# A fused attention and two-layer feed-forward kernel: the pooling of two key/value batches moves between engines, six steps change their number format, and the opening is reordered

## The chip, the cores and the metric

The kernel runs on one core of a Trainium2 chip. The metric is the device time of one execution in microseconds (us). TensorE (PE) multiplies matrices and writes to PSUM, VectorE (DVE), ScalarE (ACT) and GpSimd (POOL) work element by element, and SyncE (SP) issues every DMA of this kernel from one queue, in order.

## The reference

The core of what is computed (the first weights are called `moe_`, the second `moe2_`):

```python
k_p = k.reshape(B, H, Sp, 8, D).mean(axis=3)          # B, H, S, D = 8, 8, 576, 64; Sp = 72
v_p = v.reshape(B, H, Sp, 8, D).mean(axis=3)
scores = matmul(q, k_p.transpose(0, 1, 3, 2)) / sqrt(D)
attn = exp(scores - max); attn = attn / (sum(attn) + 1e-09)
x = matmul(attn, v_p)                                  # made (4608, 512): tokens by heads*64
h = x @ w_in1                                          # (4608, 2048)
g = where(h >= 1, h, where(h <= -1, 0, (h + 1)**2 / 4))
y = g @ w_out1                                         # (4608, 512)
out = (max(y @ w_in2, 0)**2) @ w_out2
```

## The kernel before

**Tiling.** The 4608 tokens are 36 attention tiles of 128 (`NTILE`), and 9 blocks of 512 (`NB`) in the first feed-forward layer. A block takes 16 steps (`KF`), one for each 128 of the 2048 inner columns. Step s multiplies the block's x by a column group of w_in1 (`gemm1`, L642, tile `ph`), turns the result into g (`step_ops`, L656), and two steps later (`LAG`) `gemm2` (L705) adds g times a row group of w_out1 into four accumulators `acc`. Steps are counted from 0. Here step 0 starts its `ph` matmuls at 42.07 us, step 3 at 62.72, step 8 at 104.91, step 13 at 145.82 and step 21 at 210.61. The second layer for all but the first block runs at the end, in another form, and is not touched.

**Number formats.** A float32 operand is either split into a high and a low part of type fp32r, and the product made of three matmuls (hi*hi, hi*lo, lo*hi), or multiplied whole, as float32. `whole` (L612) says which: `gemm2` of steps 0 to 15 is whole (L713, tile `gw`), every later one split (L724, tiles `gh` and `gl`). A split costs a ScalarE copy for the weight (L217), a VectorE subtraction for the weight (`wolo`, L221), a ScalarE copy of g (L687) and a VectorE subtraction of g (`gl`, L693).

**Weights.** The 32 tiles of w_in1 and w_out1 are staged by DMA (`st`, four buffers) and converted once: two ScalarE operations (L148, L151), three VectorE operations (L153, L156, L159) and one GpSimd addition (L162). Three tiles a step are converted up to step 5, then two, with a lead of 8 tiles (`LEAD`), so the last is converted around step 12. Then the second layer's weights follow in the same way (`prepare_w2`, tiles `z` and `cb`).

**Attention.** A tile of q is transposed (`unit_q`, L334): tiles 0 to 10 by TensorE (L347) out of rows of 64, tiles from `TURNED` = 11 on by VectorE (L338) after a load in pieces of 32 columns, 16 DMAs to a run of tokens (L253). Scores are made in two halves g (`unit_s`, L358): TensorE (L363), maximum on VectorE (L379), exp on ScalarE, the sum and the division by it in `norm` (L411). Attention weights of tiles 0 to 3 are transposed by TensorE (`unit_p`, L438), later ones go through DRAM. `unit_x` (L473) multiplies by the pooled v; its result is split (L485, L486) into the x of the block.

**Pooling.** The sum over 8 rows of k and v is made batch by batch (8 batches, each 4 loads of k and 4 of v, two heads a load). For batches below `ON_PE` = 3, TensorE sums in PSUM, by 8 accumulating matmuls (`unit_k` L301, `unit_v` L320). For the others GpSimd makes three additions, of 512, 256 and 128 elements (`pool_kv`, L290 and L291), and TensorE only transposes k (L306). A load buffer (`kvp`, three buffers) comes free when the pooling has read it.

**Order.** `before` (L495) lists by hand what the opening issues until step 0: k, q, s, p, v, x are the units above; `e` runs the exps that wait; `norm` divides; `head` and `tail` are the two halves of a weight's conversion; `hi` and `lo` split a weight. `slots` (L500) places the later units at half steps: batch 1's v at half steps 7 and 9, batch 2's k at 30 and 31 (step 15) and its v at 37 and 39 (steps 18 and 19). `pool_at` places GpSimd's pooling of the later batches. A scheduler then may move an instruction ahead of others on its engine where it is ready earlier, so the order in the trace is near to the program's, but not the same. The loads ahead of the loop are listed at L848 to L860.

Of the kernel before, what the change touches and what calls it, by code (L numbers as in the profile page):

```python
# [23 lines left out]

TURNED = 11

# [5 lines left out]
def pooled_attention_moe_moe(  # L32
# [59 lines left out]

    ON_PE = 3
    NK = -(-SP // TR)
# [183 lines left out]

    def pool_kv(nm, b, p):
        if b < ON_PE:  # L280
            return
        a = kv_t.pop((nm, b, p))
        if nm == "v":
            if p == 0:
                vp[b] = at.tile([SP, H, D], F32, tag="vp", name="vp")
            o = vp[b][:, 2 * p:2 * p + 2, :]
        else:
            o = kp[b, p] = at.tile([SP, 2, D], F32, tag="kp", name="kp", bufs=4)
        for w in (4 * D, 2 * D):
            nc.gpsimd.tensor_tensor(out=a[:, :, 0:w], in0=a[:, :, 0:w], in1=a[:, :, w:2 * w], op=ALU.add)  # L290
        nc.gpsimd.tensor_tensor(out=o, in0=a[:, :, 0:D], in1=a[:, :, D:2 * D], op=ALU.add)  # L291

    def unit_k(b, p0):
        pk = bank([P, 2, SP], "pk")
        for i in range(2):
            if b < ON_PE:

                a = kv_t.pop(("k", b, p0 + i)).rearrange("s h (r d) -> s h r d", r=POOL)
                for r in range(POOL):
                    for e in range(2):  # L300
                        nc.tensor.matmul(  # L301
                            out=pk[e * D:(e + 1) * D, i, :], lhsT=a[:, e, r, :], rhs=ident[:SP, :SP],
                            start=(r == 0), stop=(r == POOL - 1),
                        )
                continue
            nc.tensor.transpose(out=pk[:, i, :], in_=kp.pop((b, p0 + i)), identity=ident[:SP, :SP])  # L306
# [8 lines left out]
    def unit_v(b, p0):  # L315
        pv = bank([P, 2, 2, D], "pv")
        for i in range(2):
            a = kv_t.pop(("v", b, p0 + i)).rearrange("s h (r d) -> s h r d", r=POOL)
            for r in range(POOL):
                nc.tensor.matmul(  # L320
                    out=pv[:SP, i], lhsT=ident[:SP, :SP], rhs=a[:, :, r, :],
                    start=(r == 0), stop=(r == POOL - 1),
                )
# [34 lines left out]
    def unit_s(t, g):  # L358
# [8 lines left out]
        if g == 0:  # L367
            pn_t[t] = (
                early_pn(t) if t in (0, 1, 3) else at.tile([P, H, SP], F32, tag="pn", name="pn", bufs=1),
                at.tile([P, H, 1], F32, tag="mx", name="mx"),  # L370
            )
            if t in ON_ACT:
                sums[t] = at.tile([P, H, 1], F32, tag="sm", name="sm", bufs=3)
        pn, mx = pn_t[t]
        h = slice(4 * g, 4 * g + 4)
        s4 = pss.rearrange("p i (e s) -> p (i e) s", e=2)

        def evac():
            nc.vector.tensor_reduce(out=mx[:, h, :], in_=s4, axis=AX.X, op=ALU.max)  # L379
            if t in ON_ACT:  # L380
# [5 lines left out]
            nc.vector.tensor_tensor(  # L386
                out=pn[:, h, :], in0=s4, in1=mx[:, h, :].to_broadcast([P, 4, SP]), op=ALU.subtract
            )
            later.append(exp)

        def exp():
            if t in ON_ACT:
                for i in range(4 * g, 4 * g + 4):
                    nc.scalar.activation(
                        out=pn[:, i, :], in_=s4[:, i - 4 * g, :], func=AF.Exp, scale=exp_scale, bias=mx[:, i, :],
                        accum_out=sums[t][:, i, :],
                    )
                if g == 1:
                    norms.append(t)
                return  # L400
            nc.scalar.activation(out=pn[:, h, :], in_=pn[:, h, :], func=AF.Exp, scale=exp_scale)
            if g == 1:
# [4 lines left out]
    def early_pn(t):  # L407
        flat = pad[t % 3].rearrange("p n h c -> p (n h c)")
        return flat[:, 0:H * SP].rearrange("p (h s) -> p h s", h=H)

    def norm(t):  # L411
        pn, mx = pn_t[t] if t < TB0 else pn_t.pop(t)
        if t in sums:
            sm = sums.pop(t)
        else:
            sm = at.tile([P, H, 1], F32, tag="sm", name="sm", bufs=3)
            nc.vector.tensor_reduce(out=sm, in_=pn, axis=AX.X, op=ALU.add)

        nc.vector.tensor_scalar(out=sm, in0=sm, scalar1=1e-9, scalar2=float(POOL), op0=ALU.add, op1=ALU.mult)
        nc.vector.reciprocal(out=sm, in_=sm)  # L420
        if t < TB0:
            nc.vector.tensor_tensor(out=pn, in0=pn, in1=sm.to_broadcast([P, H, SP]), op=ALU.mult)
            return
        for i in range(NK):
            n = min(TR, SP - i * TR)
# [41 lines left out]
    def unit_x(t):  # L467
# [27 lines left out]
    before = (  # L495
        "k0,0 q0 s0,0 k0,2 q1 e s0,1 s1,0 e q2 s1,1 e v0,0 norm0 q3 s2,0 e s2,1 e head norm1 p0,0 p0,1"
        " v0,2 s3,0 e s3,1 e norm2 q4 p1,0 p1,1 norm3 x0 p2,0 p2,1 tail x1 p3,0 p3,1 head x2 tail hi0 x3 head tail"
        " lo hi1 lo head head"
    ).split()
    slots, pool_at = {}, {}  # L500
    for t in range(TB0, NTILE):
# [10 lines left out]
        if t in first_tile:  # L512
            b = first_tile.index(t)
            todo.update({2 * c - 2 + i // 2: ("k", b, i) for i in (0, 2)})
            if b < ON_PE:
                todo.update({at_v: ("v", b, i) for at_v, i in zip(((7, 9), (37, 39))[b - 1], (0, 2))})
            for i in range(2 * NP if b >= ON_PE else 0):
# [623 lines left out]
```

## Time and profile before

| | before |
|---|---|
| median of 3 runs | 1678.51 us (1674.55 to 1680.96) |
| the profiled execution, its own time | 1677.34 us |
| its span in the profile | 1675.5 us |
| busy: PE, DVE, ACT, POOL | 1642.8, 1219.0, 885.5, 315.7 us |
| mean granted TensorE clock | 0.994 |

The profile's page gives the share of the whole span: TensorE is busy for 98% of it, VectorE 73%, ScalarE 53%, GpSimd 19%. A busy time of TensorE holds short stalls inside its pipelined matmuls, so the stages have to be read one by one: busy time of each engine in a stretch, then who waited for whom in it, then the instructions in order of time.

### The profile page before, as it was taken

To read this page: it belongs to the slowest core of one execution; us is meant where nothing else is said; L and a number is where in the kernel's file an instruction comes from. 1 tells how busy PE (TensorE), PEld (TensorE's weight loads), DVE (VectorE), ACT (ScalarE), POOL (GpSimd) and SP (SyncE) were. 2 spreads that over 40 slices of the span, in tenths; PEclk is the share of its full clock that TensorE was granted. 3 is DMA by queue.
4 is the path that set the end of the run, shared out by engine and by line. 5 is a ranking of instruction groups with operands and counts; after the bars stand their busy time and mean duration, and the time that the engine had idled before them with its cause. 6 is when DMAs were issued, how large, how long until landed. Compare 5 with 4: busy or idle time off the path is not lost.

```text
span 1675.5 us, 23857 instructions
## 1 busy us (share of the span) xinstructions
PE 1642.8 (98%) x8096; PEld 1329.5 (79%) x8096; DVE 1219.0 (73%) x1963; ACT 885.5 (53%) x1603; POOL 315.7 (19%) x291
## 2 busy tenths in 40 slices
PE   8999999999999999999999999999999999999998
PEld 7666787778788787878788888888888888887886
DVE  5997478888788788888876462569557856985585
ACT  6664455656566566666566542346435533553353
POOL 1443245243514425232240000000000000000000
PEclk9999999999999999999999999999999999999999
DMA  9674534534344445443553085567687777677675
GB/s 241 168 229 156 156 83 139 163 98 142 102 150 135 119 135 171 125 129 109 181 179 117 7 299 172 170 194 231 191 253 219 207 208 239 212 209 228 194 207 133
DMA packets 276728, 284.72 MB, mean 170 GB/s; under 512 B 151168, under 2 KB 179840, under 8 KB 276608
## 3 DMA queue, kind: packets, MB, share of 16 engines
q1 hardware_dynamic: 276608, 283.21, 56.5%
q8 instruction: 65, 1.06, 0.3%
q14 instruction: 55, 0.45, 0.1%
HBM read 218.10 MB, written 65.01 MB: 169 GB/s over the span
## 4 chain that ended last, share of the span: by engine, by line
PE 71%; DVE 5%; POOL 2%; issue 1%; DMA 1%; ACT 1%; SPq 0%; DVEq 0%; POOLq 0%; ACTq 0%
PE ph L652 17%; PE acc L724 17%; PE dp L999 10%; PE cp L990 10%; PE dq L999 5%; PE cr L990 5%; PE dr L999 3%; PE cq L990 2%; PE px L473 1%; PE pss L363 1%; DMA w<-w2i 1%; DVE wolo L221 1%; DVE gl L693 1%; POOL z L162 1%; DVE wilo L221 1%
## 5 line engine op out<-in xcount | busy, mean ns | idle before, releaser
L652 PE MATMUL ph<-xhi,wihi 128*128 128x512 f32 x576 | 232.8, 404 | 2.7 <-DVE g L685 2.7
L652 PE MATMUL ph<-xhi,wilo 128*128 128x512 f32 x576 | 226.4, 393 | 0.0
L652 PE MATMUL ph<-xlo,wihi 128*128 128x512 f32 x576 | 226.1, 392 | 0.0
L947 ACT ACTIVATE gh<-g 128x512 fp32r<-128x512 f32 x224 | 139.1, 630 | 149.2 <-DVE g L1016 48.0
L724 PE MATMUL acc<-gh,wohi 128*128 128x512 f32 x512 | 206.3, 403 | 2.5 <-DVE o L738 1.5
L724 PE MATMUL acc<-gh,wolo 128*128 128x512 f32 x512 | 201.1, 393 | 3.9 <-DVE wolo L221 3.9
L724 PE MATMUL acc<-gl,wohi 128*128 128x512 f32 x512 | 200.5, 392 | 0.0
L990 PE MATMUL cp<-x,w 128*128 128x512 f32 x768 | 186.2, 390 | 0.2
L754 DVE TENSOR_TENSOR gl<-g,gh 128x512 fp32r<-128x512 f32 x224 | 151.5, 689 | 47.7 <-ACT gh L947 45.9
L990 PEld LDWEIGHTS cp<-x,w 128*128 128x128 f32 x768 | 143.9, 188 | 31.3 <-ACT s L1012 1.4
L999 PE MATMUL dp<-gh,w 128*128 128x512 f32 x512 | 161.6, 389 | 0.0
L221 DVE TENSOR_TENSOR wilo<-wi,wihi 128x512 fp32r<-128x512 f32 x144 | 114.8, 797 | 62.3 <-ACT wihi L217 62.1
L693 DVE TENSOR_TENSOR gl<-g,gh 128x512 fp32r<-128x512 f32 x144 | 116.3, 808 | 56.5 <-ACT gh L687 53.9
L217 ACT ACTIVATE wihi<-wi 128x512 fp32r<-128x512 f32 x144 | 90.1, 626 | 92.3 <-PE ph L652 91.8
L652 PEld LDWEIGHTS ph<-xhi,wihi 128*128 128x128 f32 x576 | 109.0, 190 | 32.3 <-DVE g L685 4.0
L687 ACT ACTIVATE gh<-g 128x512 fp32r<-128x512 f32 x128 | 80.5, 629 | 96.2 <-DVE g L685 95.7
L652 PEld LDWEIGHTS ph<-xhi,wilo 128*128 128x128 f32 x576 | 108.8, 189 | 23.3
L652 PEld LDWEIGHTS ph<-xlo,wihi 128*128 128x128 f32 x576 | 109.2, 190 | 22.0 <-issue 0.7
L290 POOL TENSOR_TENSOR kv<-kv 72x512 f32<-72x512 f32 x80 | 92.5, 1158 | 156.2 <-DMA kv<-in_v_dram 79.7
L1012 ACT ACTIVATE s<-cp 128x512 f32<-128x512 f32 x96 | 57.1, 595 | 118.8 <-PE cp L990 118.1
L724 PEld LDWEIGHTS acc<-gh,wolo 128*128 128x128 f32 x512 | 96.6, 189 | 23.4 <-DVE wolo L221 4.9
L724 PEld LDWEIGHTS acc<-gh,wohi 128*128 128x128 f32 x512 | 96.6, 189 | 23.3 <-DVE o L738 2.0
(142 smaller groups left out, 3206.7 us busy)
## 6 DMA issues: line engine op xcount, KB each, us to landing
w<-w2i SPq DMA_DIRECT2D x224, 256.0 KB
w<-w2o SPq DMA_DIRECT2D x224, 256.0 KB
w2i<-cb SPq DMA_DIRECT2D x32, 512.0 KB
w2o<-cb SPq DMA_DIRECT2D x32, 512.0 KB
st<-in_moe_w_out_dram SPq DMA_DIRECT2D x31, 512.0 KB
st<-in_moe_w_in_dram SPq DMA_DIRECT2D x29, 512.0 KB
pd<-pad SPq DMA_DIRECT2D x32, 384.0 KB
z<-pd SPq DMA_DIRECT2D x96, 128.0 KB
```

The lines of the kernel that those rows point to most:

```text
L217: nc.scalar.activation(out=hi, in_=src, func=AF.Copy)
L221: eng.tensor_tensor(out=lo, in0=src, in1=hi.bitcast(F32), op=ALU.subtract)
L290: nc.gpsimd.tensor_tensor(out=a[:, :, 0:w], in0=a[:, :, 0:w], in1=a[:, :, w:2 * w], op=ALU.add)
L652: nc.tensor.matmul(out=ph, lhsT=a[:, kk % a.shape[1], :], rhs=c[:, kk, :], start=(i == 0), stop=(i == 3 * KD - 1))
L687: act(out=gh, in_=g, func=AF.Copy)
L693: nc.vector.tensor_tensor(out=gl, in0=g, in1=gh.bitcast(F32), op=ALU.subtract)
L724: nc.tensor.matmul(out=o, lhsT=lhsT, rhs=rhs, start=(f == 0 and x == 0), stop=(f == KF - 1 and x == 2),)
L754: tt(out=out, in0=a, in1=b, op=ALU.subtract)
L947: act(out=hi, in_=a, func=AF.Copy)
L990: nc.tensor.matmul(out=out[0], lhsT=w[:, a, k, :], rhs=xq[b, i][c][:, k, :], start=(n == 0 and i in (1, 2, 7)), stop=(n == 5), skip_group_ ...
L999: nc.tensor.matmul(out=out[d], lhsT=w[:, a, d, :], rhs=x[c], start=(g == 0 and n == 0 and i in (1, 2, 7, 4)), stop=(g == NG - 1 and n == 2 ...
L1012: act(out=snaps[key], in_=a, func=AF.Copy)
```

## The change

Seven edits go together. (1) `ON_PE` is 2: batch 2 is pooled by GpSimd in the way of the later batches, and its slots follow: the pooling of its k is issued at half steps 16, 18, 20 and 22 (steps 8 to 11), of its v at 32, 34, 36 and 38 (steps 16 to 19). (2) Batch 0 gets two of its three additions ahead of TensorE, k on VectorE and v on GpSimd; TensorE then sums 2 rows and not 8. (3) `WHOLE` = 10: `gemm2` of steps 10 to 15 is split. (4) `TURNED` is 8: q tiles 8, 9 and 10 are loaded in pieces and turned by VectorE. (5) Tile 3's attention weights lie in two buffers of the tag `gl` that the loop doesn't use yet, and not in tile 0's, so its scores needn't wait until tile 0's weights are transposed; the small buffers `mx` and `sm` become four. (6) `before` puts the scores of all four tiles ahead of the values v and of the products x, and the first conversion later. (7) q tiles 1 to 3 are loaded ahead of v.

```diff
+WHOLE = 10
-TURNED = 11
+TURNED = 8
-    ON_PE = 3
+    ON_PE = 2
     def pool_kv(nm, b, p):
+        if b == 0:
+            a = kv_t[nm, b, p]
+            for w in (4 * D, 2 * D):
+                (nc.vector if nm == "k" else nc.gpsimd).tensor_tensor(
+                    out=a[:, :, 0:w], in0=a[:, :, 0:w], in1=a[:, :, w:2 * w], op=ALU.add
+                )
         if b < ON_PE:
             return
...
-                for r in range(POOL):
+                n = 2 if b == 0 else POOL
+                for r in range(n):
...
-                            start=(r == 0), stop=(r == POOL - 1),
+                            start=(r == 0), stop=(r == n - 1),
...
-            pn_t[t] = (
-                early_pn(t) if t in (0, 1, 3) else at.tile([P, H, SP], F32, tag="pn", name="pn", bufs=1),
...
+            if t == 3:
+                pn = [gp.tile([P, H // 2, SP], F32, tag="gl", name="pn") for _ in range(2)]
...
-        "k0,0 q0 s0,0 k0,2 q1 e s0,1 s1,0 e q2 s1,1 e v0,0 norm0 q3 s2,0 e s2,1 e head norm1 p0,0 p0,1"
-        " v0,2 s3,0 e s3,1 e norm2 q4 p1,0 p1,1 norm3 x0 p2,0 p2,1 tail x1 p3,0 p3,1 head x2 tail hi0 x3 head tail"
-        " lo hi1 lo head head"
+        "k0,0 q0 s0,0 q1 k0,2 e s0,1 s1,0 e q2 s1,1 e s2,0 q3 norm0 e s2,1 e s3,0 norm1 e s3,1 e p0,0 p0,1 norm2"
+        " v0,0 head p1,0 p1,1 v0,2 x0 norm3 p2,0 p2,1 tail head x1 q4 p3,0 p3,1 x2 tail hi0 head x3 tail lo hi1 lo head head"
...
     def whole(kind, s):
-        return kind == "o" and s < KF
+        return kind == "o" and s < WHOLE
...
     load_kv_to(NP)
-    load_q_to(2)
+    load_q_to(3)
     load_kv_to(2 * NP)
-    load_q_to(3)
```

## Rows read from the trace of the kernel before

**Rows 1.** Busy time by stretch: from:to length, each engine's busy us (instructions), PEclk, DMA share, GB/s
```profile
0.00:23.43 23.43, 18.92 (x198) 17.92 (x199) 4.00 (x12) 8.48 (x30) 1.77 (x9) 1.00 0.89 205
23.43:42.07 18.64, 15.92 (x170) 14.67 (x168) 18.37 (x37) 17.30 (x46) 5.73 (x6) 0.89 1.00 285
...
104.91:145.82 40.91, 37.26 (x163) 23.36 (x160) 37.02 (x62) 21.45 (x40) 17.70 (x14) 1.00 0.61 178
145.82:210.61 64.79, 64.79 (x422) 47.59 (x421) 36.70 (x64) 32.61 (x63) 17.78 (x18) 1.00 0.53 159
```

**Rows 2.** TensorE's waits in steps 8 to 12: waiter, releaser: us, times, longest
```profile
PE pss L363 <- DVE xlo L486: 3.7, 2, 2.3
```

**Rows 3.** Timeline of TensorE, steps 13 to 19: start, us, instruction
```profile
149.18 3.60 PE L713 MATMUL acc<-gw,wo 128*128 128x512 f32 x8
152.73 0.50 PE L652 MATMUL ph<-xhi,wihi 128*128 128x512 f32 x1
...
155.59 0.60 PE L347 MATMUL pq<-ident,q 128*128 128x128 f32 x4
156.03 3.60 PE L713 MATMUL acc<-gw,wo 128*128 128x512 f32 x8
...
163.53 2.22 PE L301 MATMUL pk<-ident,kv 72*64 72x72 f32 x64
165.68 3.70 PE L713 MATMUL acc<-gw,wo 128*128 128x512 f32 x8
...
189.29 0.48 PE L724 MATMUL acc<-gh,wohi 128*128 128x512 f32 x1
...
192.13 3.66 PE L320 MATMUL pv<-kv,ident 72*72 72x128 f32 x32
195.54 0.48 PE L652 MATMUL ph<-xhi,wihi 128*128 128x512 f32 x1
```

**Rows 4.** Timeline of TensorE, a later batch pooled by GpSimd
```profile
274.15 0.29 PE L306 MATMUL pk<-ident,kp 72*128 72x72 f32 x2
```

**Rows 5.** VectorE groups, 230 to 300 us: shapes, count, busy, mean ns, idle before
```profile
L221 DVE TENSOR_TENSOR wolo<-wo,wohi 128x512 fp32r<-128x512 f32 x11 | 11.6, 1056 | 0.3 <-ACT wohi L217 0.3
L693 DVE TENSOR_TENSOR gl<-g,gh 128x512 fp32r<-128x512 f32 x10 | 10.0, 1000 | 2.9 <-ACT gh L687 2.8
...
L338 DVE STREAM_TRANSPOSE qT<-q 128x512 f32<-128x512 f32 x3 | 2.1, 698 | 0.0
```

**Rows 6.** GpSimd groups, 230 to 300 us, and its waits there
```profile
L290 POOL TENSOR_TENSOR kv<-kv 72x512 f32<-72x512 f32 x9 | 13.5, 1497 | 30.5 <-DMA kv<-in_v_dram 25.1 <-DMA kv<-in_k_dram 5.4
L290 POOL TENSOR_TENSOR kv<-kv 72x256 f32<-72x256 f32 x9 | 7.7, 851 | 0.5
L291 POOL TENSOR_TENSOR kp<-kv 72x128 f32<-72x128 f32 x4 | 3.0, 762 | 5.7 <-PE pk L306 5.6
...
POOL kv L290 <- DMA kv<-in_v_dram: 25.1, 2, 14.5
```

**Rows 7.** Timeline of VectorE and GpSimd around 107 us
```profile
102.36 0.42 DVE L156 TENSOR_SCALAR wi<-wi 128x512 uint32<-128x512 uint32 x1
...
107.63 1.45 POOL L162 TENSOR_TENSOR wi<-low,wi 128x512 int32<-128x512 int32 x1
107.98 1.38 DVE L156 TENSOR_SCALAR wi<-wi 128x512 uint32<-128x512 uint32 x1
```

**Rows 8.** VectorE groups of conversions, steps 3 to 12, and of the second layer's weights
```profile
L156 DVE TENSOR_SCALAR wi<-wi 128x512 uint32<-128x512 uint32 x9 | 7.6, 849 | 0.2
...
L159 DVE SCALAR_TENSOR_TENSOR z<-st,z 128x512 uint32<-128x512 uint32 x2 | 1.4, 692 | 0.1
```

**Rows 9.** Busy time by stretch, clock of the opening (columns as in Rows 1)
```profile
34.12:36.42 2.30, 0.01 (x2) 0.03 (x2) 2.30 (x7) 2.30 (x6) 0.00 (x0) 1.00 1.06 268
...
38.00:48.00 10.00, 10.00 (x79) 8.29 (x76) 9.93 (x15) 6.00 (x11) 5.05 (x4) 0.50 0.31 109
```

**Rows 10.** Timeline of SyncE, a q tile loaded in pieces
```profile
216.52 4.08 SPq L253 DMA_DIRECT2D q<-in_q_dram  x9
```

More of the change, by code (lines that the diff above doesn't have):

```diff
@@ L318, in unit_v @@
             a = kv_t.pop(("v", b, p0 + i)).rearrange("s h (r d) -> s h r d", r=POOL)
-            for r in range(POOL):
+            n = 2 if b == 0 else POOL
+            for r in range(n):
                 nc.tensor.matmul(
                     out=pv[:SP, i], lhsT=ident[:SP, :SP], rhs=a[:, :, r, :],
-                    start=(r == 0), stop=(r == POOL - 1),
+                    start=(r == 0), stop=(r == n - 1),
                 )
@@ L367, in unit_s @@
         if g == 0:
[L368 to L371 removed]
+            if t == 3:
+                pn = [gp.tile([P, H // 2, SP], F32, tag="gl", name="pn") for _ in range(2)]
+            else:
+                pn = early_pn(t) if t < 2 else at.tile([P, H, SP], F32, tag="pn", name="pn", bufs=1)
+                pn = [pn[:, 0:H // 2, :], pn[:, H // 2:, :], pn]
+            pn_t[t] = pn, at.tile([P, H, 1], F32, tag="mx", name="mx", bufs=4)
             if t in ON_ACT:
[L373 to L374 removed]
+                sums[t] = at.tile([P, H, 1], F32, tag="sm", name="sm", bufs=4)
+        pn, mx = pn_t[t][0][g], pn_t[t][1]
         h = slice(4 * g, 4 * g + 4)
@@ L386, in evac @@
             nc.vector.tensor_tensor(
-                out=pn[:, h, :], in0=s4, in1=mx[:, h, :].to_broadcast([P, 4, SP]), op=ALU.subtract
+                out=pn, in0=s4, in1=mx[:, h, :].to_broadcast([P, 4, SP]), op=ALU.subtract
             )
@@ L400, in exp @@
                 return
-            nc.scalar.activation(out=pn[:, h, :], in_=pn[:, h, :], func=AF.Exp, scale=exp_scale)
+            nc.scalar.activation(out=pn, in_=pn, func=AF.Exp, scale=exp_scale)
             if g == 1:
@@ L415, in norm @@
         else:
-            sm = at.tile([P, H, 1], F32, tag="sm", name="sm", bufs=3)
-            nc.vector.tensor_reduce(out=sm, in_=pn, axis=AX.X, op=ALU.add)
+            sm = at.tile([P, H, 1], F32, tag="sm", name="sm", bufs=4)
+            for h, a in parts:
+                nc.vector.tensor_reduce(out=sm[:, h], in_=a, axis=AX.X, op=ALU.add)
         nc.vector.tensor_scalar(out=sm, in0=sm, scalar1=1e-9, scalar2=float(POOL), op0=ALU.add, op1=ALU.mult)
@@ L421, in norm @@
         if t < TB0:
-            nc.vector.tensor_tensor(out=pn, in0=pn, in1=sm.to_broadcast([P, H, SP]), op=ALU.mult)
+            for h, a in parts:
+                nc.vector.tensor_tensor(out=a, in0=a, in1=sm[:, h].to_broadcast(list(a.shape)), op=ALU.mult)
             return
+        pn = pn[2]
         for i in range(NK):
@@ L435, in unit_p @@
         pt = bank([P, 4, P], "pt")
-        pn = pn_t[t][0]
+        pn = pn_t[t][0][g]
         for i in range(4):
-            nc.tensor.transpose(out=pt[:SP, i, :], in_=pn[:, 4 * g + i, :], identity=ident)
+            nc.tensor.transpose(out=pt[:SP, i, :], in_=pn[:, i, :], identity=ident)
         def evac():
@@ L515, in pooled_attention_moe_moe @@
             if b < ON_PE:
[L516 removed]
+                todo.update({at_v: ("v", b, i) for at_v, i in zip((7, 9), (0, 2))})
             for i in range(2 * NP if b >= ON_PE else 0):
```

7 lines of the change are left out of this document (4 added, 3 removed).

## The prediction
> **What bounds the kernel now.** Read the busy times by stretch first, because the share of the whole span (TensorE 98%) hides short stalls. The change touches only the first 211 us, so three stretches matter [rows 1]. The opening, to 42.07 us: VectorE is busy for 4.00 of the first 23.43 us and ScalarE for 8.48, and then both are full (18.37 and 17.30 of 18.64): the work is there, but it starts late. Steps 8 to 12: VectorE is busy for 37.02 of 40.91 us, and TensorE waits 3.7 us for it [rows 2]; VectorE sets the pace. Steps 13 to 20: TensorE is busy for all of 64.79 us, VectorE for 36.70 [rows 1]; TensorE sets the pace. So work taken off TensorE pays in the last of the three, and work put on VectorE costs in the second. All sums are made against the profiled execution, 1677.34 us (span 1675.5 and 1.84 around it); the median is 1.17 us above that.
>
> **Steps 13 to 20, what TensorE loses.** All costs from start to start [rows 3]. Batch 2's k: 163.53 to 165.68 is 2.15 us, twice, less two pairs of transposes at 0.29 [rows 4]: 4.30 - 0.58 = 3.7 us. Its v: 192.13 to 195.54 is 3.41 us, twice: 6.8. A whole `gemm2` takes 149.18 to 152.73, 3.55 us, a split one 189.29 to 192.13, 2.84: 0.71 saved; the products of steps 11 to 15 run here, at steps 13 to 17 (step 10's at step 12): 3.6. Two q transposes (tiles 9 and 10) at 155.59 to 156.03, 0.44 each: 0.9. Together 15.0 us, leaving TensorE 49.8. VectorE gets more there: three splits of weight and g (steps 13 to 15) at 1.06 + 1.00 [rows 5], 6.2; two turns at 0.70, 1.4; and what GpSimd's pooling of v takes from it. One load is pooled in 1.50 + 0.85 + 0.76 = 3.1 us of GpSimd [rows 6], four in 12.4. What an addition on GpSimd costs VectorE is seen where both meet: the same VectorE operation takes 0.42 us alone and 1.38 beside a GpSimd addition of 1.45 [rows 7], and 0.85 on the mean of nine conversions [rows 8], twice its 0.42. So a microsecond of GpSimd costs VectorE between nothing (no operation of it there that minds) and one; I take a half, nearest to that mean: 6.2 us. VectorE then needs 36.70 + 6.2 + 1.4 + 6.2 = 50.5 us, as much as TensorE. Two engines that need 50 us each, in bursts, will not fit 50; I allow 2 us and take -12.8. The ends are -15.0 (TensorE never waits) and, with VectorE blocked for all of the 12.4, 56.7 us, -8.1.
>
> **Steps 8 to 12, what VectorE gets.** Three splits (steps 10 to 12), 6.2 us [rows 5]; one turn, 0.7; pooling of four loads of k, 12.4 us of GpSimd, half of it: 6.2. Together 13.1 us on a stretch in which VectorE idles for 40.91 - 37.02 = 3.9 [rows 1]. That leaves 9.2. Not all of it lands: VectorE also holds here the first tiles of the second layer's weights (`z`, [rows 8]), which only the second layer needs and which can slip into steps 13 to 20, and TensorE's own work shrinks by one `gemm2` (0.71) and a transpose (0.44). I take +3.5. The ends: -1, if GpSimd's additions fall where VectorE minds none and the splits fit the idle time; +15.4, if all 12.4 block it (19.3 less 3.9).
> The Trainium skill, page "SBUF — State Buffer", section "Who interferes with whom", speaks against this edit: it says that the port pair that VectorE and GpSimd share is an exclusive lock, so that the loser waits for the other's whole instruction. The pair of rows at 107 us agrees (1.38 beside 1.45), the mean of nine shows that not every operation meets one; by the rule at its hardest the term would be its upper end.
>
> **The opening.** Batch 0's k costs VectorE four times a 512- and a 256-wide addition, 4 x (0.69 + 0.42) = 4.4 us by the rows nearest in width [rows 7, 8], in the first 15 us where it idles: nothing on the path, but each k now passes through two engines, about a microsecond later for the last. For v, GpSimd's first 42 us hold only 7.5 us of work [rows 1], and four loads ask 4 x 2.35 = 9.4 [rows 6]. TensorE loses three quarters of this pooling, but it did not set the pace: from 34.12 to 36.42 it stood still with VectorE and ScalarE busy throughout [rows 9]. What can pay is that scores and exps of tiles 2 and 3 come ahead of the values and fill VectorE's and ScalarE's idle start. Both are full from 23.43 to 42.07, so the gain is what they do earlier, at best about 5 us, less GpSimd's blocking. Against it: after that 2.3 us gap TensorE's clock was granted at 0.50 for 10 us, 1.2 in place of 2.4 GHz [rows 9]; with less work TensorE pauses more, and a further stretch like that does 10 us of work as 5: +5. I take -1.5 in [-5, +5]. The new buffers for tile 3 and the order of q ahead of v cost nothing: the bytes are the same and the DMA engines are at 0.89 and 1.00 already [rows 1].
>
> **The q loads.** SyncE issues nine pieces in 4.08 us [rows 10], so 16 take 7.3 us for each of tiles 8 to 10, where one DMA stood. Queued behind them are staged weights, the loads of batch 2's k and the round trips of the attention weights. From tile 11 on the kernel loads so already; what is new is step 9, where tile 8's load meets the last staged weights and could cost up to its 7.3. I take +0.5 in [0, +7].
>
> **Sum.** -12.8 + 3.5 - 1.5 + 0.5 = -10.3: 1677.3 - 10.3 = 1667.0.
>
> **Rivals.** (a) *Everything hides.* TensorE's 15.0, the opening's 5 and -1: 1677.3 - 21 = 1656.3. For it: the later batches run in just this way. Against: VectorE has 3.9 us of idle time for 13.1 of new work.
> (b) *VectorE stays the bound through step 20.* Steps 13 to 20 give only 8.1, steps 8 to 12 cost their 9.2, the opening gives 1.5: -0.4, 1676.9. For it: 50.5 against 49.8 us above. The page's lock at its hardest leads here.
> (c) *The opening loses its clock.* The forecast with +5 in place of -1.5: 1673.5. For it: the row at 0.50 followed a gap of only 2.3 us. The Trainium skill's page "TensorE: Matmul & The Clock Gate", section "HAM oscillation", says the same of bursts with waits between them, that each next burst starts cold.
> (d) *Slower: GpSimd holds up the conversions.* Its queue is in order. A pooling that waits for its load blocks the addition that ends each weight's conversion (L162), the weight's split on VectorE waits for that, and TensorE for the split. Later batches' poolings do wait for loads, 25.1 us in two waits [rows 6], harmless there because nothing urgent is queued behind. In steps 8 to 11 the conversions are. Two such waits would land whole, as TensorE already waits for VectorE there: 1667.0 + 25.1 - 3.5 = 1688.6. Slower by more than 0.5% from about 20 us of them. Against it: batch 2's first load is issued four steps ahead, and the conversions have a lead of 8 tiles.
> (e) *The early pooling and order do nothing*, because the data's arrival sets the opening: that is the opening at 0, 1668.5, inside the forecast.
>
> **How the numbers follow.** Forecast 0.47, around 1662 to 1670; (a) 0.11; (b) 0.22; (c) 0.10; (d) 0.10. A measurement of this kernel can tell about 0.5%, 8.4 us, from no change: below 1670.1 is faster, 0.47 + 0.11 = 0.58; (b) and (c) are the same, 0.32; (d) is slower, 0.10. The range from 1656 to 1679 reaches from (a) over (b) and leaves out (d) and the outer ends of (a) and (b).
>
> **What would show it.** In the profile after, steps 13 to 20 should take about 52 us (49.8 if all hides, 57 under (b)), with VectorE over 9 tenths busy; steps 8 to 12 about 44, with longer waits for VectorE's subtractions; step 0 should start near 40.5. (c) shows as a granted clock at 0.50 well before 38 us, (d) as idle GpSimd ahead of a pooling addition in steps 8 to 11, with its conversion addition right behind. The prediction is wrong if GpSimd's additions cost VectorE far from half their time, or if the time moves behind step 21, where I expect no difference.

## The result, and the profile after

| | before | after |
|---|---|---|
| median | 1679.2 us (4 runs beside it) | 1690.38 us (1688.37 to 1691.88) |
| ratio | 1 | 1.0061 [1.0045, 1.0077] |
| the profiled execution, its span | 1677.34, 1675.5 us | 1688.37, 1686.6 us |

The change makes the kernel slower by 0.61%. The forecast was 1667.0 in 1656 to 1679, so both the sign and the range are missed. Lines have moved by two to seventeen: L652 is now L668 (`gemm1`), L724 is L740 (split `gemm2`), L221 is L223, L159 is L161, L162 is L164, L174 is L176, L290 is L299, L253 is L255.

Busy time by stretch of the kernel after, cut at its own steps 0, 8, 13 and 21 (columns as in [rows 1]; its opening is cut at 23.43 as well):

```profile
0.00:23.43 23.43, 14.29 (x96) 12.17 (x96) 11.79 (x30) 11.09 (x46) 7.01 (x15) 1.00 0.93 202
23.43:37.18 13.75, 9.77 (x104) 7.25 (x102) 13.10 (x23) 11.88 (x26) 6.11 (x7) 1.00 1.03 269
100.31:145.47 45.16, 37.30 (x164) 24.48 (x160) 42.80 (x70) 23.82 (x44) 24.33 (x21) 0.98 0.63 161
145.47:196.57 51.10, 51.10 (x246) 41.53 (x245) 36.74 (x62) 27.54 (x51) 14.40 (x15) 0.95 0.33 89
196.57:1686.00 1489.43, 1450.91 (x6777) 1185.05 (x6775) 1077.85 (x1709) 772.40 (x1368) 267.78 (x246) 0.99 0.56 169
```

The last row's counterpart in the kernel before, from its step 21:

```profile
210.61:1675.00 1464.39, 1444.12 (x6777) 1183.29 (x6775) 1062.79 (x1690) 764.34 (x1351) 245.86 (x229) 1.00 0.55 167
```

Up to step 21 the change does what was forecast, and a little more: 210.61 became 196.57. Then TensorE runs the same 6777 matmuls in both kernels and needs 25 us longer, 18.2 of it standing still (20.3 against 38.5 us), at a mean granted clock of 0.99 in place of 1.00 and with 19 more instructions on VectorE and 17 more on GpSimd. Taken from the starts of single steps, the loss from step 21 to step 159 is 23.7 us, and what comes after it in the second layer adds 1.4.

What TensorE waits for from 200 us to the end (waiter, releaser: us, times, longest), before:

```profile
PE acc L724 <- DVE wolo L221: 3.9, 2, 2.5
PE ph L652 <- DVE g L685: 2.7, 3, 1.4
PE px L473 <- DVE aT L463: 1.4, 1, 1.4
```

and after:

```profile
PE ph L668 <- DVE g L701: 10.6, 8, 3.2
PE pss L374 <- ACT kbd L321: 7.0, 1, 7.0
PE px L490 <- DVE aT L480: 6.2, 7, 3.7
PE acc L740 <- DVE wolo L223: 4.2, 3, 1.6
```

So it is no constant drag but single stalls, the longest of 7.0 us. What is new in that stretch is the second layer's weights. VectorE's groups of their conversion from step 21 on, before:

```profile
L159 DVE SCALAR_TENSOR_TENSOR z<-st,z 128x512 uint32<-128x512 uint32 x28 | 20.7, 738 | 0.2
L173 DVE TENSOR_TENSOR cb<-z,cb 128x512 fp32r<-128x512 f32 x28 | 20.0, 716 | 11.3 <-ACT cb L172 11.0
```

and after:

```profile
L161 DVE SCALAR_TENSOR_TENSOR z<-st,z 128x512 uint32<-128x512 uint32 x32 | 25.0, 782 | 0.5
L175 DVE TENSOR_TENSOR cb<-z,cb 128x512 fp32r<-128x512 f32 x32 | 25.6, 801 | 24.0 <-ACT cb L174 23.5
```

x28 against x32: the kernel before had four of the 32 tiles converted between step 11 and step 21; the kernel after has none there. And SyncE's queue, which stores what is converted, waits longer for it (270 to 950 us; SPq is SyncE's queue), before:

```profile
SPq L174 <- DVE cb L173: 35.4, 15, 10.3
SPq L174 <- POOL cb L173: 22.1, 8, 5.0
```

after:

```profile
SPq L176 <- DVE cb L175: 80.7, 21, 9.0
SPq L176 <- POOL cb L175: 42.0, 17, 8.2
SPq L176 <- DVE pn L399: 32.1, 5, 8.3
```

GpSimd's poolings, too, wait longer for the loads that SyncE issues (the same stretch), before:

```profile
POOL kv L290 <- DMA kv<-in_k_dram: 57.5, 5, 29.5
POOL kv L290 <- DMA kv<-in_v_dram: 54.5, 5, 13.5
```

after:

```profile
POOL kv L299 <- DMA kv<-in_v_dram: 83.7, 12, 19.1
POOL kv L299 <- DMA kv<-in_k_dram: 78.8, 7, 20.2
```

These are 112.0 us before and 162.5 after; in t11, the first run below, they are 111.3.

**One stall followed back.** The longest, 7.03 us at step 88, in the chain that ends in it (start, us, what; part of the steps):

```profile
609.90 0.43 SPq L255
...
615.55 0.43 SPq L255
615.98 0.04 issue
616.03 0.43 SPq L128
616.46 0.04 issue
616.50 5.25 DMA kv<-in_v_dram
621.75 0.07 issue
621.82 1.30 POOL kv L299
...
625.13 1.26 POOL z L164
626.39 1.70 POOL kv L299
628.09 1.13 POOL s L198
...
632.08 0.73 POOL z L201
632.81 0.02 issue
632.83 0.02 ACT cb L174
632.86 0.51 issue
633.37 0.61 ACT wihi L219
...
635.18 0.29 ACT kbd L321
635.48 0.04 issue
635.52 1.33 PE pss L374 x4
```

SyncE issues q pieces for 6 us (L255); a load of v stands behind them and lands at 621.75. GpSimd has waited 13.72 us for it, with the weights' additions (L164, L198 to L201) queued behind the pooling. ScalarE's copies (`cb`, L174) wait for these, and behind the copies stand `kbd` and the next weight's split, for which TensorE waits. Four in-order queues hand one late load on.

### The profile page after: what moved, and what is told of

Same layout as the page of the kernel before. It is cut to its first block, busy times and chain, and to the rows that moved or that the text cites. A ratio compares the mean times of both kernels' runs of the same rounds, so it can differ in the third digit from the quotient of the medians.

```text
span 1686.6 us, 23324 instructions
## 1 busy us (share of the span) xinstructions
PE 1625.1 (96%) x7776; PEld 1312.9 (78%) x7776; DVE 1241.5 (74%) x1988; ACT 889.1 (53%) x1610; POOL 351.1 (21%) x323
## 4 chain that ended last, share of the span: by engine, by line
PE 61%; DVE 12%; DMA 8%; POOL 6%; ACT 5%; SPq 4%; issue 4%; DVEq 0%; POOLq 0%; ACTq 0%
PE ph L668 11%; PE acc L740 11%; PE dp L1014 10%; PE cp L1005 10%; PE dq L1014 5%; PE cr L1005 5%; SPq L255 3%; PE dr L1014 3%; PE cq L1005 3%; DMA st<-in_moe_w_in_dram 2%; POOL z L164 2%; DMA kv<-in_k_dram 2%; DVE wilo L223 2%; DMA st<-in_moe_w_out_dram 1%; DVE g L701 1%
## 5 line engine op out<-in xcount | busy, mean ns | idle before, releaser
L668 PE MATMUL ph<-xhi,wihi 128*128 128x512 f32 x576 | 233.0, 405 | 11.2 <-DVE g L701 10.6
L668 PE MATMUL ph<-xlo,wihi 128*128 128x512 f32 x576 | 227.2, 395 | 0.1
L668 PE MATMUL ph<-xhi,wilo 128*128 128x512 f32 x576 | 226.5, 393 | 0.0
L962 ACT ACTIVATE gh<-g 128x512 fp32r<-128x512 f32 x224 | 139.2, 630 | 151.3 <-DVE g L1031 48.0
L740 PE MATMUL acc<-gh,wohi 128*128 128x512 f32 x536 | 217.0, 405 | 1.2 <-ACT o L752 0.7
L740 PE MATMUL acc<-gh,wolo 128*128 128x512 f32 x536 | 210.2, 392 | 4.3 <-DVE wolo L223 4.2
L740 PE MATMUL acc<-gl,wohi 128*128 128x512 f32 x536 | 209.7, 391 | 0.0
L770 DVE TENSOR_TENSOR gl<-g,gh 128x512 fp32r<-128x512 f32 x224 | 151.1, 686 | 47.6 <-ACT gh L962 46.0
L299 POOL TENSOR_TENSOR kv<-kv 72x512 f32<-72x512 f32 x96 | 115.9, 1207 | 244.8 <-DMA kv<-in_v_dram 141.0
L709 DVE TENSOR_TENSOR gl<-g,gh 128x512 fp32r<-128x512 f32 x150 | 120.3, 802 | 57.1 <-ACT gh L703 54.2
L223 DVE TENSOR_TENSOR wilo<-wi,wihi 128x512 fp32r<-128x512 f32 x144 | 122.2, 849 | 54.1 <-ACT wihi L219 53.8
L703 ACT ACTIVATE gh<-g 128x512 fp32r<-128x512 f32 x134 | 84.3, 629 | 111.6 <-DVE g L701 111.2
L668 PEld LDWEIGHTS ph<-xhi,wihi 128*128 128x128 f32 x576 | 109.4, 190 | 42.2 <-DVE g L701 14.0
L668 PEld LDWEIGHTS ph<-xhi,wilo 128*128 128x128 f32 x576 | 109.5, 190 | 23.6
L668 PEld LDWEIGHTS ph<-xlo,wihi 128*128 128x128 f32 x576 | 109.7, 190 | 22.5 <-issue 0.6
L740 PEld LDWEIGHTS acc<-gh,wolo 128*128 128x128 f32 x536 | 101.1, 189 | 25.5 <-DVE wolo L223 6.3
L740 PEld LDWEIGHTS acc<-gh,wohi 128*128 128x128 f32 x536 | 101.0, 188 | 23.9 <-DVE o L754 1.4
```

What stands on the lines that cost most here:

```text
L223: eng.tensor_tensor(out=lo, in0=src, in1=hi.bitcast(F32), op=ALU.subtract)
L668: nc.tensor.matmul(out=ph, lhsT=a[:, kk % a.shape[1], :], rhs=c[:, kk, :], start=(i == 0), stop=(i == 3 * KD - 1))
L703: act(out=gh, in_=g, func=AF.Copy)
L709: nc.vector.tensor_tensor(out=gl, in0=g, in1=gh.bitcast(F32), op=ALU.subtract)
L740: nc.tensor.matmul(out=o, lhsT=lhsT, rhs=rhs, start=(f == 0 and x == 0), stop=(f == KF - 1 and x == 2),)
L770: tt(out=out, in0=a, in1=b, op=ALU.subtract)
```

## The experiments

Each run differs from the kernel before or after only by the edit shown. Three theories were in play: **(w)** the second layer's weights are pushed behind step 21, and whoever converts them earlier loses less; **(o)** the order in the in-order queues decides, and the change shifts it from outside; **(c)** the added pooling and splits cost by themselves what is lost later. In the summaries "from 13 to 21" and so on is the difference to the kernel before of what that stretch of steps took in the profiled execution; the number of second-layer tiles converted ahead of step 21 is counted in the trace by VectorE's `z<-st,z`. Each profile is one execution, and those of one kernel spread by up to 15 us (t11: 1664.33 to 1679.24, the profiled one being the lowest), so a few us in one stretch say little by themselves.

**t11: the 48 small q loads go.**

```diff
-TURNED = 8
+TURNED = 11
```

> After, with q tiles 8 to 10 loaded in rows and transposed by TensorE again (TURNED = 11). After stood 14 to 16 us ahead of before at step 36 and then lost 26 us between steps 40 and 133. Theory A (early weights): the loss comes because the second layer's first four weight tiles are no longer prepared in steps 11 to 17 but from step 28 on, where they meet the later batches' pooling in the queues. By the instruction order of this kernel two of the four come early again (steps 18 and 22), so about half of the loss should go: 1676 to 1680 us. Theory B (order by chance): any change of the program reshuffles where the in-order queues meet, independently of how many tiles are early: the loss after step 40 could be anything from 0 to 26. Theory C (GpSimd's extra work and the three splits cost directly): they are still there, so the time stays at about 1690.

1670.03 us, ratio 0.9957 [0.9938, 0.9976]: faster than both kernels, with all of the pooling, splits and opening still in it. From 13 to 21: -12.4; behind step 21 only +4.5. Theory (c) falls. The row from its step 21 on shows it: TensorE's busy time is that of before and it idles 23.0 us, 2.7 more than before.

```profile
194.83:1662.00 1467.17, 1444.22 (x6777) 1182.97 (x6775) 1075.15 (x1704) 772.08 (x1365) 247.13 (x226) 1.00 0.55 169
```

**on3, w16: the other two loop edits go, one at a time.** `ON_PE` = 3 with the old slots of v; `WHOLE` = 16.

> After, with batch 2 pooled by TensorE again (ON_PE = 3, its v at half steps 37 and 39). TensorE gets its 10.5 us back in steps 15 to 19, so at step 36 the kernel should stand only 3 to 6 us ahead of before. Theory A: the first weight tiles come at steps 22 and 29, hardly earlier than in after, so most of the later loss stays: 1693 to 1700 us. Theory B: the later loss can be anything. Theory C: GpSimd is relieved of batch 2, the later loss goes with it: about 1675.

> After, with float32 unsplit for 16 steps again (WHOLE = 16). TensorE gets 6 x 0.71 = 4.3 us back, VectorE and ScalarE lose three pairs of operations each in steps 10 to 12 and 13 to 15; at step 36 about 11 to 14 us ahead of before. Theory A: the first tile comes at step 27, the later loss stays near 26: 1690 to 1695 us. Theory B: anything. Theory C (splits cost): no better than after either, since steps behind 16 are split in both.

on3: 1683.38, 1.0044 [1.0029, 1.006]; w16: 1686.37, 1.0053 [1.0032, 1.0075]. Without batch 2's pooling on GpSimd the gain from 13 to 21 is gone (-1.9), and 11.7 are lost behind step 21, of which 2.4 behind step 75. Without the splits: -10.9, then +15.0. Neither accounts for the loss as TURNED does.

**loop and opening: the change in two halves.** The three constants on the kernel before, and the opening's edits alone.

```diff
-    ON_PE = 3
+    ON_PE = 2
-TURNED = 11
+TURNED = 8
...
-        return kind == "o" and s < KF
+        return kind == "o" and s < 10
```

(The slots of batch 2's v go with `ON_PE`; `opening` is the kernel after with these edits undone.)

> Before, with the three edits of the loop alone (batch 2 on GpSimd, WHOLE = 10, TURNED = 8); opening as before. Without the 5 us that the opening gave at step 0, about 9 to 11 us ahead of before at step 36. Theory A: the first tile comes at step 27, the later loss stays: about 1695 us. Theory B: the later loss can be anything. If the opening's order were what hurt later, the loss would be gone: about 1669.

> The opening alone: batch 0 pooled in part by VectorE and GpSimd, scores ahead of values, q ahead of v, tile 3 in its own buffers; the three edits of the loop undone. Step 0 starts 4 to 6 us ahead of before, and with VectorE setting the pace to step 12 this should last. Theory D: the second layer's weights come at 12, 14, 18, 30, 35, from step 67 on as in before, so at most a few us are lost: 1671 to 1677 us. If the opening's gain is eaten by VectorE's stretch: 1677.

loop: 1682.45, 1.0031 [1.0018, 1.0044]; from 13 to 21 -16.0, behind +21.2. opening: 1675.79, 0.9981 [0.9965, 0.9998]; step 0 starts 7.1 us sooner, 3.5 of it is lost by step 8, and behind step 21 it wins 4.5 more. The loss behind step 21 is in the loop's half. But the two ratios make 1.0012 together and the whole change has 1.0061, so part of the loss comes only with both halves.

**t8alone: the q loads by themselves.** `TURNED` = 8 on the kernel before.

> The kernel before with TURNED = 8 alone: the 48 small q loads on SyncE's queue, none of the pooling, splits or opening. In the program's own order its second-layer conversions stand at steps 18, 22, 30, 33, 38, 41 and on as in the changed kernel with TURNED = 11, and from step 74 on as before. Theory 1 (the 48 loads cost by themselves, wherever the rest is put): it loses behind step 21 about what the kernel after loses there, 15 to 24 us, so some 1695. Theory 2 (the order that the second layer's conversions end in decides): like TURNED = 11, 3 to 6 us behind step 21 and 0 to 2 of them behind step 75; with 0 to 2 us for the loads in steps 8 to 13 and 0.9 gained on TensorE it comes to about 1680 to 1686, same as before.

1686.01, 1.0036 [1.0021, 1.0051]. Behind step 21 it loses 10.1, more than the 3 to 6 expected by order and less than 15 to 24, all of it by step 75 (behind: -0.7). The loads are a cause, but not of what the kernel after loses late.

**qact, qpool: the same 48 loads from other queues.** In the kernel after:

```diff
-                        nc.sync.dma_start(
+                        (nc.scalar if t < 11 else nc.sync).dma_start(
```

(qpool: `nc.gpsimd`.)

> After in full, with the 48 small loads of q tiles 8 to 10 issued from ScalarE's queue in place of SyncE's. VectorE still turns these tiles; SyncE's queue is free for the second layer's weights, whose first tiles come at steps 16, 19, 29 and 31 in the instruction order. Theory A with SyncE's queue as the cause: nearly as fast as with TURNED = 11, 1670 to 1676 us, a few us of ScalarE's issue time counted in. If VectorE's turning of the three tiles or the loads' small pieces were what hurts: still about 1690.

> After in full, with the 48 small loads of q tiles 8 to 10 issued from GpSimd's queue. The work is after's; the order of the second layer's weights is that of TURNED = 11 from step 30 on. Theory D: little is lost behind step 21, 4 to 8 us; what GpSimd's issuing costs in steps 9 to 16 isn't known: 1668 to 1680 us. Theory E: 1690.

qact: 1673.88, 0.9976 [0.9963, 0.9989]; qpool: 1685.66, 1.0036 [1.002, 1.0051]. From ScalarE's queue the loss behind step 21 is gone (-1.2). But the gain from 13 to 21 went too (-1.4): two second-layer tiles are now converted there, and TensorE waits 14.5 us for VectorE from 130 to 180 us. From GpSimd's queue step 13 comes 12 us later than in t11. Of these, 5.5 stand already at step 0, ahead of the first of these loads (96.4 us): TensorE's granted clock was 0.50 there from 27.1 us on. The rest comes from step 0 to step 13, where GpSimd's own work stands behind the issuing. Another 9.8 are lost behind step 21. So the cost of the 48 loads depends on the queue that issues them; their bytes are the same in all three.

**fw12, t11fw12, t11fw36: the second layer's weights earlier or later.** `first_w2` is the step from which they are prepared (28 in both kernels).

```diff
-    first_w2, wq = 2 * KF - 4, None
+    first_w2, wq = 12, None
```

> After in full, with the second layer's weights due from step 12 on and not from step 28 (one number). In the instruction order their first tiles then come at steps 15, 17, 23, 25, 32 and 34 (after: 28, 31, 36, 37). Theory A (the loss behind step 35 is the prepared weights' being late and crowded): at least 10 of the 24 us lost behind step 21 come back, 1675 to 1680 us. Theory B (every change of order reshuffles the stalls, early or late tiles don't matter): anything from 1668 to 1690, with stalls at other steps.

> After with TURNED = 11 and the second layer's weights due from step 12 on: first tiles at steps 13, 15, 19, 22, 29, 31. Theory A: the 4 to 5 us that TURNED = 11 still loses behind step 55 go too, 1664 to 1669 us, faster than both kernels. Theory B: 1665 to 1690.

> After with TURNED = 11 (1670 us), and the second layer's weights due from step 36 on. In the instruction order the first four tiles come at steps 22, 29, 33 and 35 (18, 22, 30, 33 with TURNED = 11 alone) and six, not eight, are done by step 50; they end more crowded. Theory A: the loss behind step 35 comes back in part, 1677 to 1688 us. Theory B: no rule, anything from 1665 to 1690.

fw12: 1776.36, 1.058 [1.0561, 1.06]; t11fw12: 1690.52, 1.0072 [1.0052, 1.0092]; t11fw36: 1679.39, 1.0003 [0.9991, 1.0016]. fw12 missed by far the most; t11fw36 lies in the ranges of both theories. In fw12 and t11fw12 tiles are converted earlier (two and three ahead of step 21), yet 102.5 and 17.0 us are lost behind it. Theory (w) in its plain form falls. Waits of TensorE and of SyncE's queue in fw12, 200 us to the end and to 950 us:

```profile
PE px L490 <- DVE aT L480: 77.7, 17, 11.0
SPq L176 <- DVE cb L175: 151.4, 16, 20.5
```

In this order the weights' stores stand in SyncE's queue ahead of the round trips of the attention weights and wait up to 20.5 us for a conversion; TensorE then waits for the transposed weights `aT`. The granted clock is lower, too: 0.963 on the mean of the run, 0.994 in the kernel before. An estimate from these two puts up to 0.031 x 1774 = 55 us of the loss on the clock.

**bheld, t11held: the second layer's loads keep their place in the program.** The load of a second-layer tile is queued behind the last store of attention weights that the program has issued, in the kernel before and in t11.

```diff
-            nc.sync.dma_start(out=p_d[t], in_=pad[t % 2])
+            mark[0] = nc.sync.dma_start(out=p_d[t], in_=pad[t % 2]).ins
...
-            stage_w(kind, 1, f)
+            with tc.issue_after(mark[0]):
+                stage_w(kind, 1, f)
```

> Before, none of the change in it; the loads of the second layer's weights are queued on SyncE behind the latest store of attention weights, so the scheduler can't issue them ahead of their place. Their first tiles then come at steps 27, 30, 36, 37, 42 and 44, as in after, and not at 11, 12, 14 and 17. Theory D (the time behind step 21 is set by the order of the queues, which the change shifted from outside): this kernel loses behind step 21 like after, 15 to 24 us, 1692 to 1701 us. Theory E (the change's own added work on VectorE and GpSimd costs it): nothing of it is here, 1674 to 1681.

> After with TURNED = 11 (1670 us), and the second layer's weight loads held in their place in the same way. Theory D: up to step 21 as fast as it was, 15 us ahead, then a loss of 15 to 24 us: 1684 to 1692 us. Theory E: the change's work is the same as in TURNED = 11 alone: 1670.

bheld: 1705.32, 1.0166 [1.0149, 1.0183]; t11held: 1700.62, 1.0131 [1.0116, 1.0146]. bheld has nothing of the change, no tile ahead of step 21, gains nothing there (-0.2 from 13 to 21) and loses 27.7 behind. t11held loses 32.2, t11 4.5: 27.7 again. TensorE's waits of bheld (200 us to the end):

```profile
PE ph L654 <- DVE g L687: 19.4, 13, 5.9
```

So a loss of the size that was sought comes without the change, by moving the second layer's loads alone. The edit also alters the order of all later tiles, so it does not part (w) from (o).

**stact, stpool: the stores leave SyncE's queue.** In the kernel after, the stores of L176 from ScalarE's and from GpSimd's queue.

```diff
-        nc.sync.dma_start(out=w2c[kind][g][:, n:n + 2], in_=c.bitcast(F32))
+        nc.scalar.dma_start(out=w2c[kind][g][:, n:n + 2], in_=c.bitcast(F32))
```

> The kernel after with the stores of the second layer's converted weights on ScalarE's queue in place of SyncE's; the 48 q loads and all else stay. If a store that waits on SyncE's queue for its conversion is the root of the stalls (q pieces, kv loads and z fetches wait behind it), the waits of SyncE's queue for those stores go, and with them most of the 23.7 us behind step 21: 1667 to 1674. If the root is GpSimd's and ScalarE's in-order work (additions of the conversion, poolings that wait for data), the stalls stay or move and the time stays at 1685 to 1692; a store that waits on ScalarE's queue for GpSimd's addition would then hold up ScalarE's own work as well, and it could come out above that.

> The kernel after with the same stores on GpSimd's queue. By the first theory (stores waiting on SyncE's queue) as the run with ScalarE's queue, 1667 to 1674. By the other the stalls stay: 1685 to 1692, or above where a store that waits for ScalarE's copy holds up a pooling on GpSimd.

stact: 1699.62, 1.0106 [1.0077, 1.0134]; stpool: 1715.2, 1.0201 [1.0174, 1.0229]. SyncE waits no more for these conversions, and the time is longer: 32.6 and 47.5 us are lost behind step 21. From 21 to 60 these kernels convert 12 and 13 tiles, the kernel after 10, before 8. So the waits of SyncE's queue for these stores are not the root. The preparation is faster without them and the time longer; that the faster preparation is what costs is not shown, as the stores now stand in ScalarE's or GpSimd's own queue.

**pre9, pre14, t11pre14: the first four tiles are moved back.** They are prepared from step 9 or 14 on, two pieces a step; the other 28 keep their place in the program.

```diff
             upto = min(n_w2, -(-n_w2 * (s + 1 - first_w2) // (NS0 - 4 - first_w2)))
+            upto = max(upto, min(18, 2 * (s - 13)))
```

(Under `if s >= 14`; pre9 with 9 and 8; t11pre14 is pre14 with TURNED = 11.)

> The kernel after with nothing changed but the place of the second layer's first four weight tiles: they are prepared from step 9 on, two pieces a step, and the other 28 keep the steps that they have in the kernel after. In the trace four tiles (of 32) should then be converted before step 21, as in the kernel before (there 4, in the kernel after none). If the change's loss behind step 21 is the work of these four tiles, pushed into a stretch that has no room for it, most of the 23.7 us comes back: 0 to 8 lost behind step 21, while steps 8 to 20 give back 4 to 9 us of VectorE's time (the four tiles take 9.0 us of VectorE there in the kernel before). Sum 1668 to 1678. If it is the order of the later queues (from step 40 on unchanged here, pairs of tiles close together as in the kernel after), the stalls at steps 46 to 133 stay, 12 to 24 us behind step 21, and it comes out at 1686 to 1696.

> The same with the four tiles from step 14 on, so that they miss steps 8 to 13, where VectorE sets the pace, and fall on steps 16 to 24, where it was busy for 36.74 of 51.10 us in the kernel after. By the first theory 0 to 10 us are lost behind step 21 and 0 to 5 in steps 13 to 20: 1666 to 1677. By the second 12 to 24 us behind step 21: 1685 to 1694.

> TURNED = 11 in the kernel after (the fast one, 1670.0, with one tile before step 21 and 4.5 us lost behind it), and the first four tiles from step 14 on as in the run before. Its tiles stand in the program's order at steps 13, 15, 18, 19, then 35, 38, 42 and on as in the kernel whose q loads go by ScalarE's queue. Both theories give little loss behind step 21, -2 to 4 us; the first puts 0 to 5 us on steps 13 to 20. 1666 to 1674; above 1676 neither accounts for it.

pre9: 1686.63, 1.0048 [1.003, 1.0066]; pre14: 1693.98, 1.0094 [1.0063, 1.0125]; t11pre14: 1679.21, 1.0006 [0.9989, 1.0023]. pre9 has four tiles ahead of step 21 and loses 2.3 us behind it instead of 23.7. But steps 13 to 20 now take 11.5 us more than before, not 13.7 less:

```profile
138.87:215.15 76.28, 59.98 (x261) 47.53 (x261) 60.76 (x92) 41.70 (x77) 33.82 (x30) 0.84 0.44 135
```

with TensorE's waits there

```profile
PE px L490 <- DVE aT L480: 13.7, 3, 7.3
```

VectorE is busy 60.76 us of this stretch, against 36.74 in the kernel after. t11pre14, too, has four tiles there and gains 0.4 us from 13 to 21 where t11 gains 12.4. Over steps 8 to 20 together pre9 takes 8.6 us more than before, the kernel after 9.4 less, so the four tiles come at 18.1 us there, and by the same reckoning at 13.7 in t11pre14 against t11; 4 to 9 had been expected. Up to some 10 us of it, by an estimate, is TensorE's clock, which was at 0.50 from 143.6 to 153.8 us, around the wait of 7.3 us that ended at 147.38: at 0.84 on the mean the stretch lacks 76.28 x 0.16 = 12.2 us, in the kernel after, at 0.95, 51.10 x 0.05 = 2.6. From step 13 to 21 t11pre14 has 0.89 and t11 1.00.

pre14 got only two tiles ahead of step 21; the next two fall behind it, where 8 us go by step 26. From step 42 on VectorE's instruction order has its conversions at the steps of the kernel after, every one. And the stall of step 88 is back (timeline of TensorE: start, us, instruction [idle before]), after first, then pre14:

```profile
635.52 1.33 PE L374 MATMUL pss<-kbd,qT 128*128 128x144 f32 x4 [7.03 <-ACT kbd L321]
```

```profile
639.56 1.33 PE L374 MATMUL pss<-kbd,qT 128*128 128x144 f32 x4 [7.18 <-ACT kbd L321]
```

**All runs side by side.** Differences to the kernel before, us:

| run | tiles ahead of step 21 | 13 to 21 | 21 to 75 | 75 to 159 |
|---|---|---|---|---|
| opening | 3 | -0.2 | -6.0 | +1.5 |
| qact | 2 | -1.4 | -2.5 | +1.3 |
| t11pre14 | 4 | -0.4 | -0.9 | +2.4 |
| t11 | 1 | -12.4 | +4.3 | +0.2 |
| qpool | 2 | -4.3 | +6.7 | +3.1 |
| t8alone | 1 | -1.1 | +10.8 | -0.7 |
| on3 | 0 | -1.9 | +9.3 | +2.4 |
| pre9 | 4 | +11.5 | -1.9 | +4.3 |
| loop | 0 | -16.0 | +16.3 | +4.8 |
| w16 | 0 | -10.9 | +7.2 | +7.8 |
| after | 0 | -13.7 | +10.8 | +12.9 |
| pre14 | 2 | -12.4 | +14.3 | +13.0 |
| bheld | 0 | -0.2 | +10.4 | +17.4 |
| t11fw36 | 0 | -14.1 | -3.9 | +17.7 |
| t11held | 0 | -13.2 | +11.5 | +20.6 |
| t11fw12 | 3 | -4.2 | +7.9 | +9.1 |
| stact | 0 | -13.7 | +24.3 | +8.3 |
| stpool | 0 | -14.3 | +31.1 | +16.4 |
| fw12 | 2 | -7.6 | +57.0 | +45.5 |

*Behind step 75* the order decides. The first seven runs of the table have their conversions, in VectorE's instruction order from step 74 on, at the steps of the kernel before (74, 77, 83, 86, 90 and so on), and lose -0.7 to +3.1, whatever else is in them. The kernel after and pre14 share another order (74, 75, 79, 84, 86 and so on) and lose 12.9 and 13.0. Of the edits, the 48 loads on SyncE's queue and batch 2's pooling on GpSimd bring this order about together: without the one (t11), without the other (on3, t8alone) or with the loads on ScalarE's queue (qact) the late loss is -0.7 to +2.4. Both at once are not enough: loop, w16 and pre9 have them, with orders of their own, and lose 4.8, 7.8 and 4.3. Nor are they needed: bheld, which lacks both, and t11held, which lacks the loads, share an order close to that of the kernel after (75, 79, 84, 86, 91, 93 in all three) and lose 17.4 and 20.6. *From 13 to 21* the gain and the early tiles exclude each other: of the runs with both loop edits that pay there (`ON_PE` and `WHOLE`), those with no or one tile gain 12.4 to 16.0, those with two to four between 7.6 and less than nothing. pre14 is the exception, with two tiles and 12.4. Part of this is the clock again: it is 0.89 in that stretch of qact and t11pre14 and 0.84 in pre9, but 0.96 in pre14. *From 21 to 75* the trend is the reverse one, three or four tiles: -6.0 to -0.9, none: +7.2 to +31.1, but with exceptions on both sides (t11fw12, t11fw36), so how much of these 10.8 us is the four tiles' work and how much its order stays open. Open also stays which coincidence starts each single stall; one was followed.

## Why the prediction was wrong, step by step

**The opening** (-1.5 in [-5, +5]): -4.9, step 0 at 37.18 instead of near 40.5. The mechanism held, the size was too small: VectorE does 11.79 us of work in the first 23.43 us, where it did 4.00 [rows 1], ScalarE 11.09 against 8.48. The granted clock is 1.00 up to step 0, so rival (c) did not come in this execution; the stretch at 0.50 of [rows 9] has no like ahead of step 0. But it came in others. Sixteen of the profiled kernels have the opening's edits. In ten of them the clock is at 1.00 nearly up to step 0, which starts at 34.95 to 37.97 us. In six (w16, qpool, stpool, fw12, t11held, t11fw36) it falls to 0.50 between 24.5 and 27.8 us, and step 0 starts at 41.23 to 43.58, so that little or nothing of the gain is left. In w16:

```profile
26.70:41.23 14.53, 13.42 (x87) 9.71 (x85) 8.56 (x17) 9.29 (x19) 2.58 (x2) 0.50 1.02 285
```

**Steps 8 to 12 and the q loads** (+3.5 and +0.5): +4.2, 45.16 us where about 44 was forecast. The sum held, its reason less. Waits for the subtraction `xlo` did not grow, 3.7 us in [rows 2] became 0.6; one wait of 5.0 us for `aT` took their place. VectorE has 42.80 us of work there, not 37.02 + 13.1: the two second-layer tiles of the kernel before, 3.8 us, have left, and GpSimd's additions cost less than half their time: 42.80 + 3.8 - 37.02 - 6.9 for the splits and the turn leaves 2.7 us for the 12.4 of k.

**Steps 13 to 20** (-12.8): -13.7, 51.10 us where 52 was forecast. TensorE is busy for all of it, and that at a granted clock of 0.95: behind the wait of 5.05 us for `aT`, which ended at 143.57 us, it was at 0.50 (1.2 of 2.4 GHz) up to 150.4 us, or 0.77 on the mean of the first 10.53 us:

```profile
145.47:156.00 10.53, 10.53 (x40) 8.57 (x39) 8.22 (x14) 4.46 (x8) 1.97 (x3) 0.77 0.18 32
```

At full clock the same work would have taken 10.53 x 0.23 = 2.4 us less. The Trainium skill, page "TensorE: Matmul & The Clock Gate", section "HAM oscillation", tells of bursts that start cold behind waits; the row agrees. That the size came out right is in part luck: the 2 us allowed for two full engines went to the clock, and VectorE was far from full. It was to be busy for 50.5 us, over 9 tenths, and was for 36.74. The splits' work is there (`wolo` x8 against x2, `gl` x8 against x5, together 6.3 us more for the 6.2 of the sum) and both q turns (1.4). GpSimd's blocking, put at 6.2, shows as 1.4 at most: the mean of `wilo` rose from 749 to 832 ns, of `wolo` from 684 to 776, eight each, while that of `gl` fell from 847 to 710. So the sign that the prediction named, additions that cost VectorE far from half their time, came in both stretches. And the two second-layer tiles of this stretch, 5.2 us with their `cb`, are not in it any more.

**Behind step 21** ("where I expect no difference"): +23.7, and 1.4 more in the second layer. This is the step that failed, a term put at nothing. The prediction had seen that VectorE's 37.02 and 36.70 us hold the first tiles of the second layer's weights, and that they "can slip into steps 13 to 20"; it gave that slip no price and did not ask whether they would come there. They did not: the kernel after converts its first at step 28. The program lists them from step 28 on in both kernels (`first_w2`); in the kernel before, the scheduler had moved four of them ahead, two into steps 8 to 12 and two into steps 13 to 20, where VectorE idled for 28.1 of 64.79 us. That the change left them no room is not shown. VectorE still idles for 14.4 of the 51.10 us from step 13 to 21, all four had taken 9.0 us of VectorE (3.8 + 5.2), and pre14 has two of them there and keeps 12.4 us of the gain. Put back by hand, all four are dear: from step 8 to 21 pre9 is 18.1 us slower than the kernel after, which is twice the 9.4 gained there. With none of them there the kernel after lost 10.8 us up to step 75 and, by the order that then follows, 12.9 behind it. How much of the 10.8 is the tiles' work stays open, as t11fw36, with none ahead of step 21 either, wins 3.9 in that stretch.

**The q loads** (+0.5 in [0, +7]) are the other term that failed. They were costed by what stood behind them at step 9, which was a local price. With batch 2's pooling, the time they take of SyncE's queue changes the order of weights, loads and stores for the next hundred steps: 1690.4 us with them on SyncE's queue, 1673.9 from ScalarE's, 1670.0 without, so 20.4 us hang on them.

**Rivals.** (d) had the right kind of mechanism, a pooling that waits for its load with the weights' additions queued behind it, 13.72 us long in the stall shown, but at step 88 and on the second layer's weights; in steps 8 to 12 no pooling waited for a load. [Rows 6] had shown two such waits, 25.1 us in all, and the prediction called them harmless "because nothing urgent is queued behind". That was true of that stretch only; `z` additions share the queue. (c), put at 0.10, came in six of sixteen profiled executions with the new opening, though not in that of the kernel after. (a), (b) and (e) speak of steps 0 to 20 and did not decide.

The better kernel is t11, the change without TURNED = 8: it keeps 12.4 us of the gain from 13 to 21, at 1670.0 us, close to the forecast for the whole.

## What to carry to other kernels

When a change fills an engine's idle time, list what else was using that time, also work that is not due for a long time: it has no wait in the trace of before, and where it goes is part of the price. A few dozen small DMAs on the one queue that issues everything can cost far more than what stands right behind them (here 20.4 us where 0.5 was forecast), as they can move every later load and store. Where several in-order queues hand work to each other, a difference of 1% may be a matter of order alone: undo the cheapest part of a change first, and try its DMAs from another queue, before the idea is given up.

## What the hardware showed that was not expected

Taking a wait off a queue made it worse: with 155 us of SyncE's waits for stores gone from its queue (80.7 + 42.0 + 32.1, 270 to 950 us) and the stores issued from ScalarE's or GpSimd's, the kernel became 9 and 25 us slower. The granted clock of the same opening differed from profile to profile: at 0.50 for 14 to 18 us ahead of step 0 in six, at 1.00 in ten for all but the last microsecond. And stalls repeat almost exactly: with the same order of conversions, two kernels that reach step 75 4 us apart lost 12.9 and 13.0 us from there on, with a wait of 7.03 and 7.18 us at the same matmul.
